# The first stage's channels stored in pairs and the slot spectra stored slot by slot, in a fused FFT, soft-MoE and SwiGLU kernel

## The chip, the core and the metric

The kernel runs on 1 core of one Trainium2 chip. The metric is device time in microseconds. Three runs of the kernel before took 1813.24, 1824.9 and 1827.48 us; their median is 1824.9 us. The engines are TensorE (PE; its weight loads are listed apart, as PEld), VectorE (DVE), ScalarE (ACT), GpSimd (POOL) and SyncE (SP), which issues most DMAs.

## The reference

Eight sequences of 3072 tokens of width 256 pass through three layers in turn.

```
X = rfft(x, axis=1)                             # x: [8, 3072, 256]
Yr = Xr @ w_r - Xi @ w_i + b_r ;  Yi = Xr @ w_i + Xi @ w_r + b_i
Y  = softshrink(Yr, 0.01) + 1j * softshrink(Yi, 0.01)
y  = irfft(Y)                                   # then [24576, 256]

logits = y @ phi                                # phi: [256, 32], 8 experts x 4 slots
d = softmax(logits, over all tokens);  c = softmax(logits, over the 32 slots)
slot_out[e] = relu((d.T @ y)[e] @ w1[e]) @ w2[e]
z = c @ slot_out

out = (silu(z @ w_gate) * (z @ w_val)) @ w_out  # 256 -> 1536 -> 256
```

All of it is in float32. The softmax over tokens runs over all eight sequences.

## The kernel before, in words

The 3072-point transform is split as 96 x 32. The first phase goes over the 8 batches b. For each:

- **Stage A** (`stage_a`): 16 products (L625) of the input with a 96-point transform; each gives one PSUM bank of 128 channels x 32 x 16 columns. A 32 x 32 block transpose on VectorE (L630) turns each bank into the tile `chan`, which has one slab of 128 columns per channel.
- **Stage C** (`stage_c`): per channel one product (L647) whose weights (the stationary operand) are that channel's 128 columns of `chan`; ScalarE and VectorE split the results into a high and a low part (L666, L669, L672, L675, L684, L688).
- **Stage B** (`stage_b`, L742): the mixing matrices w_r and w_i in three products per pair, on high and low parts. `after_b` does the shrinking (L795 to L814).
- **Stage Q** (`stage_q`): the logits' spectrum (L840), a transpose of it (L851), a transpose of Y in place (L856), and 16 DMAs (L866) that spread Y for the slots.
- **`logits`**: from the spectrum of 32 slots to logits over tokens, in two halves of 16 slots. Per half: product (L900), rotation by twiddle factors (L886, two multiplications), joins (L921), transpose (L929), product (L969), maximum (L978) and a copy kept for later (L990). The tile `vpad` is the transposes' source; it holds 24 rows of the ordinary pairs (`v_cj`) and, in row 24, the real pair (frequencies that have a real transform), copied in by L946.
- **`slots`**: the reverse way, from the exponentials to their spectrum: product (L1062), transpose (L1070), rotation (L886 on VectorE, the cross part on POOL or VectorE), joins (L1098), main product (`d_mm`, L1109), and for the real pair a small product of its own (`sd_mm`, L1119) in a PSUM bank of its own. `evac` copies the main product to SBUF (L1127) and then the real pair's 32 x 32 values over its place (L1130). Then `slot_mm` (L1163) forms the slots' inputs.
- **`combine`**: the softmax over slots, stored to DRAM.

In `vpad`, in the transposed tiles and in the logits, the slot is the innermost index: a half is 16 words in every 32.

The order of all this is not written by hand. Every step is a task handed to `Plan.add` with an engine, an estimated duration, a rank and the data it reads and writes. `Plan.run` is a list scheduler: among the tasks that can start it takes the one with the earliest estimated start, ties by rank, and emits it. The table `SHIFT` holds an offset of the rank for each kind of task. PSUM and SBUF buffers are rings with a fixed number of places (`ch`: 3 banks) and count as dependencies. Each engine then executes its own list strictly in order.

After the last batch, the expert weights that arrive by DMA are used (`after_slots`: L1513, L1536), and then the last layer runs over all 24576 tokens (L1614 to L1646), from about 742 us to the end.

Of the kernel before, what the change touches and what calls it, by code (L numbers as in the profile page):

```python
# [22 lines left out]
R1 = 96  # L23
# [9 lines left out]
def dft_tables():  # L33
# [64 lines left out]
    for i in range(R2):  # L98
        if i == 0:
            spi[0, 0, 0, :] = 1.0 / n  # L100
            spi[0, 1, 0, :] = alt2 / n
            spf[0, :, 0, 0] = 1.0 / n
            spf[0, :, 1, 0] = alt2 / n
# [7 lines left out]
        spf[h, :, 1, i] = -w * np.sin(a)  # L111

# [47 lines left out]
for _n, _w in (  # L160
# [59 lines left out]
    "slots.join": -7.11,  # L220
    "slots.sd_mm": -8.76,
    "slots.d_mm": -3.64,
# [44 lines left out]
    "slots.join'": 40.67,  # L267
    "slots.sd_mm'": 0.52,
    "slots.d_mm'": 14.24,
# [136 lines left out]
def kernel(  # L406
# [79 lines left out]
    def phase1():  # L486
# [39 lines left out]

        chan = apool.tile([128, 56, 128], F32, name="chan")

        twc = sm("twc").rearrange("p (c j) -> p c j", c=2)
        tws = sm("tws").rearrange("p (c j) -> p c j", c=2)  # L530
        inv = sm("inv").rearrange("p (m k) -> p m k", m=6)
# [3 lines left out]
        gf = sm("gf")  # L535
        v_cj = vpad[:, 0:24].rearrange("p (c j) s -> p c j s", c=2)

# [78 lines left out]
        def stage_a(b, p, rank):  # L616
            dq, dd = divmod(p, 4)
            dh, d0 = dq // 2, (dq % 2) * 64 + dd * 16
            kq = ("xq", b, dq) if b else ("x0", dh)
            kt, ka = ("tt", b, dh), ("ac", "a", b, p)  # L620
            d1 = dd * 16 if b else d0

            def mm():
                pt = bank(ka, [128, R2, 16], "ac")
                nc.tensor.matmul(  # L625
                    out=pt, lhsT=fwd[:, 8 - 8 * dh:136 - 8 * dh], rhs=T[kq][:, :, d1:d1 + 16], start=True, stop=True
                )

            def turn():
                nc.vector.transpose(  # L630
                    out=chan[:, 24 * dh:24 * dh + 32, d0:d0 + 16].rearrange("p j d -> p d j"),
                    in_=T[ka].rearrange("p n d -> p d n"),
                )

            add("PE", 0.86, rank, mm, r=["f", kq, kt], w=[ka], new=[("ac", ka)] + ([("tt", kt)] if p % 8 == 0 else []))
            add("DVE", 0.6, rank, turn, r=[ka], w=[(*kt, p)])

        def stage_c(b, g, hb, dh, rank):
# [51 lines left out]
            def last_mm():  # L690
                if dh == 0:
                    bank(kz, [128, 2, 2], "ch")
                nc.tensor.matmul(out=T[kz][:, dh], lhsT=chan[:, 32 * dh, :], rhs=sm("last"), start=True, stop=True)

# [189 lines left out]
        def times(eng, out, v, tw):  # L884
            e = nc.vector if eng == "DVE" else nc.gpsimd
            e.tensor_tensor(out=out, in0=v, in1=tw.unsqueeze(3).to_broadcast([128, 2, NSC, 16]), op=ALU.mult)  # L886

        half = [slice(0, 16), slice(16, 32)]

        def logits(b, k):  # L890
# [16 lines left out]
            def rot(h):  # L907
                def go():
                    if h == 0:
                        sb(chp, kp2, [128, 2, NSC, 32], "p2")  # L910
                    v = T["ch", "v", b, h]
                    times("DVE", v_cj[:, :, :, half[h]], v, twc)
                    times("DVE", T[kp2][:, :, :, half[h]], v, tws)

                return go

            def join(h):
                def go():
                    for c in range(2):
                        v = v_cj[:, c, :, half[h]]  # L920
                        nc.vector.tensor_add(out=v, in0=v, in1=T[kp2][:, 1 - c, :, half[h]])  # L921

                return go

            def turn(h):
                def go():
                    if h == 0:
                        sb(chp, kvt, [128, 32, 32], "vt")
                    nc.vector.transpose(  # L929
                        out=T[kvt][:, :, half[h]].rearrange("p n s -> p s n"),  # L930
                        in_=vpad[:, :, half[h]].rearrange("p m s -> p s m"),
                    )

# [11 lines left out]
            def sp_out():  # L945
                nc.scalar.activation(out=vpad[0:64, 24, :], in_=T[ks], func=AF.Copy)  # L946
# [19 lines left out]
            def l_mm(h):  # L966
                def go():
                    pt = bank(("ch", "l", b, h), [R1, 32, 16], "ch")
                    nc.tensor.matmul(out=pt, lhsT=gi, rhs=T[kvt][:, :, half[h]], start=True, stop=True)  # L969

                return go

            def colmax(h):
                def go():
                    if h == 0:
                        sb(chp, m96, [R1, 32], "m96")
                    pt = T["ch", "l", b, h].rearrange("p n s -> p s n")
                    nc.vector.reduce_max(out=T[m96][:, half[h]], in_=pt, axis=AX.X)  # L978

# [75 lines left out]
        def slots(b, k):  # L1055
# [10 lines left out]
            def turn(h):  # L1066
                def go():
                    if h == 0:
                        sb(chp, t2, [128, 32, 32], "vt")
                    nc.vector.transpose(  # L1070
                        out=T[t2][:, :, half[h]].rearrange("p m s -> p s m"),
                        in_=T["ch", "t", b, h].rearrange("p n s -> p s n"),
                    )

                return go

            def t4(h):
                return T[t2][:, 0:24, half[h]].rearrange("p (c j) s -> p c j s", c=2)

            def rot(h):  # L1080
                def go():
                    times("DVE", v_cj[:, :, :, half[h]], t4(h), twc)

                return go

            def cross(h):
                def go(eng):
                    if h == 0:
                        sb(chp, kp2, [128, 2, NSC, 32], "p2")
                    times(eng, T[kp2][:, :, :, half[h]], t4(h), tws)  # L1090

                return go

            def join(h):
                def go():
                    for c in range(2):
                        v = v_cj[:, c, :, half[h]]
                        nc.vector.tensor_sub(out=v, in0=v, in1=T[kp2][:, 1 - c, :, half[h]])  # L1098

                return go  # L1100

            ksd, d = ("ch", "sd", b), ("p2", "d", b)

            def d_mm(h):
                def go():
                    pt = bank(("ch", "d", b, h), [128, 2, NSC, 16], "ch")
                    for c in range(2):
                        for i in range(2):
                            nc.tensor.matmul(  # L1109
                                out=pt[:, c], lhsT=fwc[2 * c + i], rhs=v_cj[:, i, :, half[h]],  # L1110
                                start=(i == 0), stop=(i == 1),
                            )

                return go

            def sd_mm():
                pt = bank(ksd, [32, 2, 32], "ch")
                for c in range(2):
                    nc.tensor.matmul(  # L1119
                        out=pt[:, c], lhsT=spf[0:64, c, :], rhs=T[t2][0:64, 24, :], start=True, stop=True  # L1120
                    )

            def evac(h):
                def go():
                    if h == 0:
                        sb(chp, d, [128, 2, NSC, 32], "p2")
                    nc.scalar.activation(  # L1127
                        out=T[d][:, :, :, half[h]], in_=T["ch", "d", b, h], func=AF.Copy, scale=2.0 / SEQ
                    )
                    nc.scalar.activation(out=T[d][0:32, :, 0, half[h]], in_=T[ksd][:, :, half[h]], func=AF.Copy)  # L1130

                return go

            for h in range(2):
# [8 lines left out]
                add("DVE", 0.54, k + 0.01 * h, join(h), r=[(*kp2, h)], w=[("vp", h)])  # L1143
            add("PE", 0.1, k + 0.2, sd_mm, r=["csm", (*t2, 0), (*t2, 1)], w=[ksd], new=("ch", ksd))
            for h in range(2):
                kd = ("ch", "d", b, h)
                add("PE", 1.32, k + 0.2 + 0.01 * h, d_mm(h), r=["csm", ("vp", h)], w=[kd], new=("ch", kd), after=[ksd])
                add(
                    "ACT", 0.6, k + 0.2 + 0.01 * h, evac(h), r=[kd, ksd], w=[(*d, h)],
                    new=("p2", d) if h == 0 else None,  # L1150
# [553 lines left out]
```

## Time and profile before

| | |
|---|---|
| median of 3 runs | 1824.9 us (1813.24 to 1827.48) |
| profiled execution | 1821.86 us, its span 1819.8 us |
| TensorE busy in the span | 1719.7 us (94%) |
| VectorE busy | 1378.2 us (76%) |
| ScalarE busy | 984.8 us (54%) |
| POOL busy | 274.0 us (15%) |
| mean granted TensorE clock | 0.979 of full speed |

Busy time is the union of an engine's instructions. Averages over the span mix the first phase (to about 665 us), the change-over (to about 740 us) and the last layer, so the rows below are taken by stretch. A float32 product appears as two matmul records and two weight loads.

### The profile page before, as it was taken

The page shows a single profiled execution, that of the slowest core. Times are in us where ns is not written, and L with a number is a line of the kernel's source. Part 1 is how long each engine was busy: PE and PEld are TensorE (multiplying, and loading weights), DVE is VectorE, ACT ScalarE, POOL GpSimd, SP SyncE. Part 2 cuts the span into 40 slices and gives each one's busy share as a digit, 9 for nine tenths or more (in the row PEclk, how much of TensorE's full clock was granted, in tenths as well). Part 3 has the DMA queues.
Part 4 walks back from the last instruction along what each step waited for, and adds up shares of the span by engine and source line. Part 5 has one row for each costly group of instructions (what it writes and reads, how often), then busy time and mean ns, then how long its engine had stood idle before and what let it go on. Part 6 is the DMA issues. An engine that isn't in the chain of part 4 may idle for free.

```text
span 1819.8 us, 23377 instructions
## 1 busy us (share of the span) xinstructions
PE 1719.7 (94%) x8234; PEld 1291.9 (71%) x8234; DVE 1378.2 (76%) x2219; ACT 984.8 (54%) x1849; POOL 274.0 (15%) x257
## 2 busy tenths in 40 slices
PE   6999898997898996999999999999999999999998
PEld 3665655655565673688888888888888888888886
DVE  5798888898888872677777777777777777777776
ACT  1554545553553641565656565656565656565654
POOL 1324343442433342000000000000000000000000
PEclk8999989998999998999999999999999999999999
DMA  8355553755365569511211211211211212111111
GB/s 171 72 106 123 106 118 82 140 105 125 93 122 111 151 211 282 121 24 23 50 24 24 50 24 24 50 23 24 50 24 36 37 24 45 28 24 24 26 27 30
DMA packets 258916, 134.44 MB, mean 74 GB/s; under 512 B 197392, under 2 KB 246256, under 8 KB 258800
## 3 DMA queue, kind: packets, MB, share of 16 engines
q1 hardware_dynamic: 252944, 120.37, 31.3%
q0 software_dynamic: 5856, 12.58, 3.7%
q8 instruction: 65, 1.06, 0.3%
q14 instruction: 51, 0.42, 0.1%
HBM read 69.99 MB, written 37.75 MB: 59 GB/s over the span
## 4 chain that ended last, share of the span: by engine, by line
PE 74%; DVE 14%; DMA 4%; SPq 3%; issue 2%; ACT 2%; POOL 1%; DVEq 0%; ACTq 0%; POOLq 0%
PE o L1639 44%; PE pg L1614 7%; PE pv L1615 7%; PE pb L742 5%; PE ac L625 3%; PE ac L647 3%; DVE chan L630 3%; DMA w2s<-in_moe_w_dram 2%; DVE yt L856 1%; SPq L866 1%; DVE xg L669 1%; PE ch L840 1%; DVE vpad L1098 1%; DMA yi<-yt 1%; DVE vt L1070 1%
## 5 line engine op out<-in xcount | busy, mean ns | idle before, releaser
L1639 PE MATMUL o<-hh,wo 128*128 128x512 f32 x2304 | 722.5, 394 | 0.0
L1619 DVE TENSOR_TENSOR h<-sg,pv 128x512 f32<-128x512 f32 x576 | 394.0, 684 | 271.7 <-ACT sg L1617 270.1
L1617 ACT ACTIVATE sg<-pg 128x512 f32<-128x512 f32 x576 | 344.5, 598 | 421.8 <-PE pg L1614 421.8
L1639 PEld LDWEIGHTS o<-hh,wo 128*128 128x128 f32 x2304 | 434.3, 188 | 100.7
L1639 PE MATMUL o<-hl,wo 128*128 128x512 f32 x1152 | 453.9, 394 | 0.0
L1627 DVE TENSOR_TENSOR hl<-h,hh 128x512 fp32r<-128x512 f32 x576 | 393.4, 683 | 0.2
L1626 ACT ACTIVATE hh<-h 128x512 fp32r<-128x512 f32 x576 | 359.4, 624 | 0.7 <-DVE h L1619 0.7
L1639 PEld LDWEIGHTS o<-hl,wo 128*128 128x128 f32 x1152 | 216.1, 188 | 52.0 <-DVE hl L1627 0.2
L1614 PE MATMUL pg<-cst,gstk 96*128 96x512 f32 x576 | 228.3, 396 | 0.0
L1615 PE MATMUL pv<-cst,gstk 96*128 96x512 f32 x576 | 226.3, 393 | 0.7 <-DVE gstk L1601 0.7
L742 PE MATMUL pb<-xg,wh 128*128 128x512 f32 x384 | 150.5, 472 | 11.7 <-ACT yt L795 6.8
L814 POOL TENSOR_TENSOR yt<-r,yt 128x512 f32<-128x512 f32 x93 | 120.5, 1295 | 263.5 <-ACT yt L805 167.5
L630 DVE STREAM_TRANSPOSE chan<-ac 128x512 f32<-128x512 f32 x128 | 130.1, 1065 | 30.2 <-PE ac L625 30.1
L1566 POOL DMA_DIRECT2D cst<-c_scr x24 | 13.5, 571 | 813.1 <-PE pv L1615 799.7
L625 PE MATMUL ac<-xq,fwd 96*128 96x512 f32 x224 | 115.8, 628 | 14.5 <-DVE chan L630 9.2
L1615 PEld LDWEIGHTS pv<-cst,gstk 96*128 96x128 f32 x576 | 109.7, 190 | 27.3 <-DVE gstk L1601 1.6
L1614 PEld LDWEIGHTS pg<-cst,gstk 96*128 96x128 f32 x576 | 108.1, 188 | 24.4 <-issue 0.5
L647 PEld LDWEIGHTS ac<-cm,chan 128*128 128x128 f32 x768 | 96.7, 196 | 19.6 <-DVE chan L630 8.2
L647 PE MATMUL ac<-cm,chan 128*128 128x128 f32 x768 | 101.2, 282 | 5.9 <-DVE chan L630 3.3
L742 PEld LDWEIGHTS pb<-xg,wh 128*128 128x128 f32 x384 | 69.2, 197 | 51.1 <-issue 18.9
L669 DVE TENSOR_TENSOR xg<-ac,xg 128x512 fp32r<-128x512 f32 x96 | 64.8, 680 | 24.1 <-ACT sf L672 21.2
L625 PEld LDWEIGHTS ac<-xq,fwd 96*128 96x128 f32 x224 | 38.9, 194 | 58.7 <-DVE chan L630 33.4
(147 smaller groups left out, 1683.1 us busy)
## 6 DMA issues: line engine op xcount, KB each, us to landing
yi<-yt SPq DMA_DIRECT2D x384, 64.0 KB, 2.1
out_dram<-ob SPq DMA_DIRECT2D x192, 128.0 KB, 2.8
xq<-in_x_dram SPq DMA_DIRECT2D x28, 768.0 KB, 7.4
cst<-c_scr POOLq DMA_DIRECT2D x24, 384.0 KB, 6.7
w1s<-in_moe_w_dram SPq DMA_DIRECT2D x8, 1024.0 KB, 7.2
w2s<-in_moe_w_dram SPq DMA_DIRECT2D x8, 1024.0 KB, 10.3
w_scr<-cv SPq DMA_DIRECT2D x48, 128.0 KB, 2.2
x<-in_x_dram SPq DMA_DIRECT2D x2, 1536.0 KB, 15.0
```

The lines of the kernel that those rows point to most:

```text
L625: nc.tensor.matmul(out=pt, lhsT=fwd[:, 8 - 8 * dh:136 - 8 * dh], rhs=T[kq][:, :, d1:d1 + 16], start=True, stop=True)
L630: nc.vector.transpose(out=chan[:, 24 * dh:24 * dh + 32, d0:d0 + 16].rearrange("p j d -> p d j"), in_=T[ka].rearrange("p n d -> p d n"),)
L647: nc.tensor.matmul(out=pt[:, :, q:q + 2, i // 2, :], lhsT=chan[:, 32 * dh + j, :], rhs=cm[:, j, :].rearrange("p (c h k) -> p c h k", c=2, ...
L742: nc.tensor.matmul(out=pt, lhsT=w[:, dh, m, es], rhs=xx, start=m != 1 and dh == 0 and n == 0, stop=dh == 1 and n == 2, skip_group_check=True,)
L814: e.tensor_sub(out=part(), in0=quarters(T[kr]), in1=part())
L1614: nc.tensor.matmul(out=pg, lhsT=gstk[:, 0, f * 128:(f + 1) * 128], rhs=rhs, start=True, stop=True)
L1615: nc.tensor.matmul(out=pv, lhsT=gstk[:, 1, f * 128:(f + 1) * 128], rhs=rhs, start=True, stop=True)
L1617: nc.scalar.activation(out=sg, in_=pg, func=AF.Silu)
L1619: nc.vector.tensor_mul(out=h, in0=sg, in1=pv)
L1626: nc.scalar.activation(out=hh, in_=h, func=AF.Copy)
L1627: nc.vector.tensor_sub(out=hl, in0=h, in1=hh.bitcast(F32))
L1639: nc.tensor.matmul(out=po_t[0][k], lhsT=w[:, f % 4, k * 128:(k + 1) * 128], rhs=a, start=(f == 0 and m == 0), stop=(f == NF - 1 and m == 2 ...
```

## The change

Three things are done.

1. The tile `chan` becomes `[128, 28, 128, 2]`: the values of channels 2m and 2m+1 lie side by side. The transpose of stage A writes them in pairs; stage C takes one channel's weights with a step of two words.
2. In `logits` and `slots` the slot becomes the outer index: a half is 16 slots of 32 words without gaps, the transposes L929 and L1070 write without gaps, the rotation multiplies 16 x 24 words, and the joins handle 16 runs of 12 words. The logits in PSUM are also slot by slot; the copy L990 reads them across.
3. `sd_mm`, its bank and its tasks go. Its two products are done per half inside `d_mm` and added in the same PSUM bank, with the constants `spf` scaled to fit. The second copy of `evac` goes; the first reads its bank across.

The inverse product of batch b is given an order constraint after the `d_mm` of batch b - 1.

```diff
@@ dft_tables
-            spf[0, :, 0, 0] = 1.0 / n
+            spf[0, :, 0, 0] = 1.0 / w / n
...
-        spf[h, :, 0, i] = w * np.cos(a)
+        spf[h, :, 0, i] = np.cos(a)
@@ SHIFT: the two entries "slots.sd_mm" and "slots.sd_mm'" go
@@ tiles
-        chan = apool.tile([128, 56, 128], F32, name="chan")
+        chan = apool.tile([128, 28, 128, 2], F32, name="chan")
...
-        v_cj = vpad[:, 0:24].rearrange("p (c j) s -> p c j s", c=2)
+        v_cj = vpad[:, :, 0:24].rearrange("p s (c j) -> p s c j", c=2)
@@ stage_a
-                    out=chan[:, 24 * dh:24 * dh + 32, d0:d0 + 16].rearrange("p j d -> p d j"),
+                    out=chan[:, 12 * dh:12 * dh + 16, d0:d0 + 16, :].rearrange("p j d i -> p d j i"),
@@ stage_c
-                        out=pt[:, :, q:q + 2, i // 2, :], lhsT=chan[:, 32 * dh + j, :],
+                        out=pt[:, :, q:q + 2, i // 2, :], lhsT=chan[:, 16 * dh + j // 2, :, j % 2],
@@ times
-            e.tensor_tensor(out=out, in0=v, in1=tw.unsqueeze(3).to_broadcast([128, 2, NSC, 16]), op=ALU.mult)
+            e.tensor_tensor(out=out, in0=v, in1=tw.unsqueeze(1).to_broadcast([128, 16, 2 * NSC]), op=ALU.mult)
@@ logits
-                    v = T["ch", "v", b, h]
-                    times("DVE", v_cj[:, :, :, half[h]], v, twc)
+                    v = T["ch", "v", b, h].rearrange("p c j s -> p s (c j)")
+                    times("DVE", vpad[:, half[h], 0:24], v, twc)
...
-                        v = v_cj[:, c, :, half[h]]
-                        nc.vector.tensor_add(out=v, in0=v, in1=T[kp2][:, 1 - c, :, half[h]])
+                        v = v_cj[:, half[h], c]
+                        nc.vector.tensor_add(out=v, in0=v, in1=T[kp2][:, half[h], NSC * (1 - c):NSC * (2 - c)])
...
-                        out=T[kvt][:, :, half[h]].rearrange("p n s -> p s n"),
-                        in_=vpad[:, :, half[h]].rearrange("p m s -> p s m"),
+                    nc.vector.transpose(out=T[kvt][:, half[h]], in_=vpad[:, half[h]])
...
-                add("PE", 1.32, k + 0.01 * h, inv_mm(h), r=["csm"] + qts, w=[kv], new=("ch", kv))
+                add("PE", 1.32, k + 0.01 * h, inv_mm(h), r=["csm"] + qts, w=[kv], new=("ch", kv), after=[("ch", "d", b - 1, 1)] * (b > 0))
...
-                    nc.scalar.activation(out=T[ls][:, :, half[h]], in_=T["ch", "l", b, h], func=AF.Copy)
+                    nc.scalar.activation(out=T[ls][:, :, half[h]], in_=T["ch", "l", b, h].rearrange("p s n -> p n s"), func=AF.Copy)
@@ slots
-                        out=T[t2][:, :, half[h]].rearrange("p m s -> p s m"),
-                        in_=T["ch", "t", b, h].rearrange("p n s -> p s n"),
+                    nc.vector.transpose(out=T[t2][:, half[h]], in_=T["ch", "t", b, h].rearrange("p n s -> p s n"))
...
+                    for c in range(2):
+                        nc.tensor.matmul(
+                            out=pt[0:32, c, :, 0], lhsT=spf[0:64, c, :], rhs=T[t2][0:64, half[h], 24],
+                            start=False, stop=True, skip_group_check=True,
+                        )
...
-                    nc.scalar.activation(out=T[d][0:32, :, 0, half[h]], in_=T[ksd][:, :, half[h]], func=AF.Copy)
...
-            add("PE", 0.1, k + 0.2, sd_mm, r=["csm", (*t2, 0), (*t2, 1)], w=[ksd], new=("ch", ksd))
...
-                add("PE", 1.32, k + 0.2 + 0.01 * h, d_mm(h), r=["csm", ("vp", h)], w=[kd], new=("ch", kd), after=[ksd])
+                add("PE", 1.42, k + 0.2 + 0.01 * h, d_mm(h), r=["csm", ("vp", h), (*t2, h)], w=[kd], new=("ch", kd))
```

## Rows read from the trace of the kernel before

**Rows 1.** Windows: start:end, length, then busy us (instructions) per engine, granted clock, DMA.

```profile
core 0: us, PE busy (x) PEld busy (x) DVE busy (x) ACT busy (x) POOL busy (x), PEclk, DMA share, GB/s
26.00:665.00 639.00, 578.40 (x3151) 384.30 (x3151) 543.71 (x878) 324.52 (x669) 244.38 (x214) 0.95 0.53 115
665.00:740.00 75.00, 56.60 (x457) 35.27 (x453) 27.08 (x76) 14.37 (x26) 18.82 (x19) 0.91 1.00 281
742.00:1819.00 1077.00, 1071.40 (x4607) 867.69 (x4606) 794.98 (x1247) 642.36 (x1150) 10.01 (x18) 1.00 0.19 31
```

**Rows 2.** Chain of waits, 26 to 665 us: shares of the chain by engine and line.

```profile
by line: PE pb L742 14.8%; PE ac L625 9.4%; PE ac L647 9.1%; DVE chan L630 7.5%; issue 5.6%; DVE yt L856 4.2%; DVE xg L669 3.3%; PE ch L840 2.3%; SPq L866 2.1%; DVE vpad L1098 2.1%; DMA yi<-yt 2.1%; DVE vt L1070 2.0%; DVE yt L798 2.0%; DVE 
```

**Rows 3.** Waits of TensorE, 26 to 665 us: total us, times, longest us.

```profile
PE ac L625 <- DVE chan L630: 10.9, 14, 2.6
PE ch L969 <- DVE vt L929: 7.3, 5, 2.1
...
PE ac L647 <- DVE chan L630: 3.3, 4, 2.2
PE ch L969 <- DVE cv L1261: 3.1, 1, 3.1
```

**Rows 4.** Groups of VectorE by shape: busy us, mean ns of one, idle before them.

```profile
L630 DVE STREAM_TRANSPOSE chan<-ac 128x512 f32<-128x512 f32 x128 | 130.1, 1065 | 30.2 <-PE ac L625 30.1
...
L1646 DVE STREAM_TRANSPOSE ob<-o 128x512 f32<-128x512 f32 x96 | 62.7, 690 | 2.3 <-PE o L1639 2.3
L856 DVE STREAM_TRANSPOSE yt<-yt 128x1024 f32<-128x1024 f32 x48 | 58.5, 1219 | 6.1 <-PE ch L840 5.8
...
L929 DVE STREAM_TRANSPOSE vt<-vpad 128x512 f32<-128x512 f32 x16 | 18.6, 1161 | 0.8
...
L1070 DVE STREAM_TRANSPOSE vt<-ch 128x512 f32<-128x512 f32 x16 | 16.9, 1058 | 1.6 <-PE ch L1062 1.6
...
L978 DVE TENSOR_REDUCE m<-ch 96x16 f32<-96x512 f32 x16 | 10.6, 669 | 3.8 <-PE ch L969 3.7
L851 DVE STREAM_TRANSPOSE qt<-ch 128x256 f32<-128x256 f32 x24 | 10.3, 428 | 3.0 <-PE ch L840 3.0
...
L1219 DVE STREAM_TRANSPOSE vt<-ls 96x1024 f32<-96x1024 f32 x8 | 9.8, 1225 | 3.0 <-POOL ls L1215 3.0
```

**Rows 5.** Instructions of line L1098: min/median/max ns.

```profile
L1098 DVE TENSOR_TENSOR vpad<-vpad,p x32: 291/438/2062, 139.1 to 687.4; 128x192 f32<-128x192 f32 x32
```

**Rows 6.** Timeline of TensorE at 239 us: start, us, operation, idle before.

```profile
239.61 3.78 PE L625 MATMUL ac<-xq,fwd 96*128 96x512 f32 x4 [2.59 <-DVE chan L630]
```

**Rows 7.** Window of 240 to 250 us, columns as in the first group.

```profile
240.00:250.00 10.00, 10.00 (x24) 4.87 (x24) 7.59 (x11) 2.11 (x3) 2.99 (x2) 0.52 0.31 74
```

**Rows 8.** Timeline of TensorE and its weight loads: two stage C passes.

```profile
515.98 1.86 PEld L647 LDWEIGHTS ac<-cm,chan 128*128 128x128 f32 x16 [0.23 <-DVE chan L630]
...
641.18 1.95 PE L647 MATMUL ac<-cm,chan 128*128 128x128 f32 x16
```

**Rows 9.** Groups of ScalarE by shape, columns as for VectorE.

```profile
L684 ACT ACTIVATE sg<-sf 128x256 fp32r<-128x256 f32 x96 | 37.4, 413 | 27.6 <-PE pb L742 24.6 <-DVE sf L675 2.7
...
L1267 ACT ACTIVATE cvi<-cvi 128x256 f32<-128x256 f32 x36 | 15.9, 442 | 37.7 <-DVE cv L1262 33.9 <-issue 3.8
```

**Rows 10.** Timeline of TensorE at 138 us.

```profile
138.38 0.31 PE L1119 MATMUL ch<-vt,csm 64*32 64x32 f32 x4 [0.93 <-DVE vt L1070]
```

**Rows 11.** Groups of ScalarE: the copies out of PSUM in logits and slots.

```profile
L990 ACT ACTIVATE ls<-ch 96x512 f32<-96x512 f32 x16 | 9.5, 591 | 30.6 <-DVE m L978 30.5
...
L1127 ACT ACTIVATE p<-ch 128x384 f32<-128x384 f32 x16 | 7.8, 489 | 19.5 <-DVE vpad L1098 8.6 <-PE ch L1109 8.3 <-PE pb L742 2.5
...
L1130 ACT ACTIVATE p<-ch 32x32 f32<-32x32 f32 x16 | 3.0, 186 | 0.5
```

**Rows 12.** Groups of VectorE: the logits' rotation.

```profile
L886 DVE TENSOR_TENSOR p<-ch,csm 128x384 f32<-128x384 f32 x16 | 8.8, 549 | 0.0
```

**Rows 13.** Timeline of TensorE at 724 us.

```profile
724.59 4.99 PE L1536 MATMUL po<-w2s,h1t 128*32 128x256 f32 x58 [9.80 <-DMA w2s<-in_moe_w_dram]
```

More of the change, by code (lines that the diff above doesn't have):

```diff
@@ L101, in dft_tables @@
             spi[0, 1, 0, :] = alt2 / n
-            spf[0, :, 0, 0] = 1.0 / n
-            spf[0, :, 1, 0] = alt2 / n
+            spf[0, :, 0, 0] = 1.0 / w / n
+            spf[0, :, 1, 0] = alt2 / w / n
             continue
@@ L220 @@
     "slots.join": -7.11,
-    "slots.sd_mm": -8.76,
     "slots.d_mm": -3.64,
@@ L267 @@
     "slots.join'": 40.67,
-    "slots.sd_mm'": 0.52,
     "slots.d_mm'": 14.24,
@@ L525, in phase1 @@
         fwd = apool.tile([R1, FWD], F32, name="fwd")
-        chan = apool.tile([128, 56, 128], F32, name="chan")
-        twc = sm("twc").rearrange("p (c j) -> p c j", c=2)
-        tws = sm("tws").rearrange("p (c j) -> p c j", c=2)
+        chan = apool.tile([128, 28, 128, 2], F32, name="chan")
+        twc = sm("twc")
+        tws = sm("tws")
         inv = sm("inv").rearrange("p (m k) -> p m k", m=6)
@@ L692, in last_mm @@
                     bank(kz, [128, 2, 2], "ch")
-                nc.tensor.matmul(out=T[kz][:, dh], lhsT=chan[:, 32 * dh, :], rhs=sm("last"), start=True, stop=True)
+                nc.tensor.matmul(out=T[kz][:, dh], lhsT=chan[:, 16 * dh, :, 0], rhs=sm("last"), start=True, stop=True)
             def last_out():
@@ L909, in go @@
                     if h == 0:
-                        sb(chp, kp2, [128, 2, NSC, 32], "p2")
-                    v = T["ch", "v", b, h]
-                    times("DVE", v_cj[:, :, :, half[h]], v, twc)
-                    times("DVE", T[kp2][:, :, :, half[h]], v, tws)
+                        sb(chp, kp2, [128, 32, 2 * NSC], "p2")
+                    v = T["ch", "v", b, h].rearrange("p c j s -> p s (c j)")
+                    times("DVE", vpad[:, half[h], 0:24], v, twc)
+                    times("DVE", T[kp2][:, half[h]], v, tws)
                 return go
@@ L945, in sp_out @@
             def sp_out():
-                nc.scalar.activation(out=vpad[0:64, 24, :], in_=T[ks], func=AF.Copy)
+                nc.scalar.activation(out=vpad[0:64, :, 24], in_=T[ks], func=AF.Copy)
             for h in range(2):
                 kv = ("ch", "v", b, h)
-                add("PE", 1.32, k + 0.01 * h, inv_mm(h), r=["csm"] + qts, w=[kv], new=("ch", kv))
+                add("PE", 1.32, k + 0.01 * h, inv_mm(h), r=["csm"] + qts, w=[kv], new=("ch", kv), after=[("ch", "d", b - 1, 1)] * (b > 0))
                 if h == 0:
@@ L967, in go @@
                 def go():
-                    pt = bank(("ch", "l", b, h), [R1, 32, 16], "ch")
-                    nc.tensor.matmul(out=pt, lhsT=gi, rhs=T[kvt][:, :, half[h]], start=True, stop=True)
+                    pt = bank(("ch", "l", b, h), [R1, 16, 32], "ch")
+                    nc.tensor.matmul(out=pt, lhsT=gi, rhs=T[kvt][:, half[h]], start=True, stop=True)
                 return go
@@ L976, in go @@
                         sb(chp, m96, [R1, 32], "m96")
-                    pt = T["ch", "l", b, h].rearrange("p n s -> p s n")
-                    nc.vector.reduce_max(out=T[m96][:, half[h]], in_=pt, axis=AX.X)
+                    nc.vector.reduce_max(out=T[m96][:, half[h]], in_=T["ch", "l", b, h], axis=AX.X)
                 return go
@@ L1069, in go @@
                         sb(chp, t2, [128, 32, 32], "vt")
-                    nc.vector.transpose(
-                        out=T[t2][:, :, half[h]].rearrange("p m s -> p s m"),
-                        in_=T["ch", "t", b, h].rearrange("p n s -> p s n"),
-                    )
+                    nc.vector.transpose(out=T[t2][:, half[h]], in_=T["ch", "t", b, h].rearrange("p n s -> p s n"))
                 return go
             def t4(h):
-                return T[t2][:, 0:24, half[h]].rearrange("p (c j) s -> p c j s", c=2)
+                return T[t2][:, half[h], 0:24]
             def rot(h):
                 def go():
-                    times("DVE", v_cj[:, :, :, half[h]], t4(h), twc)
+                    times("DVE", vpad[:, half[h], 0:24], t4(h), twc)
                 return go
@@ L1088, in go @@
                     if h == 0:
-                        sb(chp, kp2, [128, 2, NSC, 32], "p2")
-                    times(eng, T[kp2][:, :, :, half[h]], t4(h), tws)
+                        sb(chp, kp2, [128, 32, 2 * NSC], "p2")
+                    times(eng, T[kp2][:, half[h]], t4(h), tws)
                 return go
@@ L1096, in go @@
                     for c in range(2):
-                        v = v_cj[:, c, :, half[h]]
-                        nc.vector.tensor_sub(out=v, in0=v, in1=T[kp2][:, 1 - c, :, half[h]])
+                        v = v_cj[:, half[h], c]
+                        nc.vector.tensor_sub(out=v, in0=v, in1=T[kp2][:, half[h], NSC * (1 - c):NSC * (2 - c)])
                 return go
-            ksd, d = ("ch", "sd", b), ("p2", "d", b)
+            d = ("p2", "d", b)
             def d_mm(h):
                 def go():
-                    pt = bank(("ch", "d", b, h), [128, 2, NSC, 16], "ch")
+                    pt = bank(("ch", "d", b, h), [128, 2, 16, NSC], "ch")
                     for c in range(2):
@@ L1109, in go @@
                             nc.tensor.matmul(
-                                out=pt[:, c], lhsT=fwc[2 * c + i], rhs=v_cj[:, i, :, half[h]],
-                                start=(i == 0), stop=(i == 1),
-                            )
-                return go
[L1116 to L1121, printed above, removed]
+                                out=pt[:, c], lhsT=fwc[2 * c + i], rhs=v_cj[:, half[h], i],
+                                start=(i == 0), stop=(i == 1), skip_group_check=True,
+                            )
+                    for c in range(2):
[3 more added lines that the diff above has]
+                        )
+                return go
             def evac(h):
@@ L1127, in go @@
                     nc.scalar.activation(
-                        out=T[d][:, :, :, half[h]], in_=T["ch", "d", b, h], func=AF.Copy, scale=2.0 / SEQ
+                        out=T[d][:, :, :, half[h]], in_=T["ch", "d", b, h].rearrange("p c s j -> p c j s"),
+                        func=AF.Copy, scale=2.0 / SEQ,
                     )
-                    nc.scalar.activation(out=T[d][0:32, :, 0, half[h]], in_=T[ksd][:, :, half[h]], func=AF.Copy)
                 return go
```

6 lines of the change are left out of this document (2 added, 4 removed).

## The prediction

> **What bounds the kernel now.** I read the busy time by stretch first [rows 1]. The long last stage, 742 to 1819 us, keeps TensorE busy for 1071.4 of 1077 us, and no line of it is edited: the change can only act before it. From 26 to 665 us the eight batches of the first phase run, and two engines are nearly full at once: TensorE 578.4 and VectorE 543.7 of 639 us. Neither can be named the bound alone. Between them, 665 to 740, the DMA engines are busy all the time (share 1.00).
>
> The chain of waits inside 26 to 665 us [rows 2] says how the two share the end. TensorE has the largest pieces (L742 14.8%, L625 9.4%, L647 9.1%), but the stage A transpose L630 alone holds 7.5%, and the slots' transpose L1070 2.0%. The waits of TensorE [rows 3] agree: the longest single total is for L630, and the third transpose, L929, costs it 7.3 us in 5 waits.
>
> **The transposes.** In the groups of VectorE [rows 4] the same operation of 512 columns has two prices: 690 ns where it writes without gaps (L1646), and 1065 (L630), 1161 (L929) and 1058 (L1070) where each word lands 128 or 512 bytes from the last. From L851 (256 columns, 428 ns) and L1646 a gapless one costs 166 ns + 1.02 ns per column; the 1024 columns of L1219 and L856, read from SBUF, fit that at 1219 to 1225, so the source does not matter. It is the write that costs, not the gapped read: the reduction L978 reads PSUM at 64 byte steps, as L630 and L1070 do, and takes 669 ns for 512, no more than gapless work of that size. A gapped write costs (1065 - 166)/512 = 1.76 ns per word.
>
> - L929 and L1070 get outputs without gaps: I take 690, so 0.47 and 0.37 us less, 16 times each, 13.4 us of VectorE. The other end is nothing gained.
> - L630 now writes two words side by side and then jumps 1024 bytes. No row has pairs. The upper bound is 1065, the lower 690. In between: were the 0.73 ns extra per jump simply added, a pair would pay it once, 1.02 + 0.37 = 1.39 ns per word, 878 ns. I take 690: a jump costs 1.76 ns in all, and the two words need 2.04 ns in any case, so it fits under them; and the joins L1098, which jump after every 16 words, have a fastest execution of 291 ns for 192 words [rows 5], under the 362 of 166 + 1.02 x 192, so a jump by itself is not charged. That is 128 x 0.375 = 48 us of VectorE.
>
> The Trainium skill, "SBUF — State Buffer", section "Door 1: The DMA port swizzle", says that accesses which keep moving to a new 16-byte line pay, and that two hits on a line are enough to hide it. By that rule the pair is at 690 and the sum is the one below; without any such effect L630 stays at 1065 and the sum loses 16.9 us. No row here shows which.
>
> **What of it lies on the path.** L630: 7.5% of 639 us is 47.9 us on the chain; 375/1065 of that is 16.9. L1070: 2.0% is 12.8, times 368/1058 is 4.4. L929 is not named in the chain's line; of the 7.3 us in 5 waits each can lose at most 0.47, so 2.4. Together 23.7 us. With the order of work unchanged the chain cannot shrink by more, and other chains lie close behind, since TensorE is already busy 90.5% of the stretch. I take four fifths, 19 us: it would leave TensorE busy 578/620 = 93%. Half is the pessimistic end.
>
> **The clock.** TensorE loses speed after long waits. At 239.6 us it had waited 2.59 us for L630, and four stage A matmul records took 3.78 us [rows 6]; the granted clock from 240 to 250 is 0.52, the lower level of 1.2 GHz [rows 7]. Over 26 to 665 us the mean is 0.95 [rows 1], so 0.05 x 639 = 32 us of full-speed time is lost. Shorter waits for L630 give some back. Bounds 0 to 16 us (half); I take 4, as the two waits for L630 (10.9 + 3.3 us) and the one for L929 are 21.5 of the 60.6 us in which TensorE is idle, and they shorten by about a third.
>
> **The weights of stage C.** L647 loads its weights from the channel tile, now with a step of 8 bytes. No weight load of this trace has a step. Today 16 records take 1.86 us on the load side and 1.95 on the matmul side [rows 8], 0.11 us each: load and matmul are level, nothing would hide a slower load. Lower bound: no change. Upper bound: twice the load, 0.11 us x 768 = 85 us of TensorE. I take no change, by the nearest row with such a step: ScalarE squares 256 words in place at 8 byte steps in 442 ns, against 413 for 256 words without gaps [rows 9].
>
> **The small matmuls of the slots.** One set of four records becomes two per batch, 0.31 us each [rows 10]: 8 x 0.31 = 2.5 us of TensorE at most; below, 0, if they run beside others. TensorE holds some 40% of the chain: +1 us. They wait only for the transposes that the main product needed already. The new order constraint (inverse product after the last batch's spectra) changes nothing: both lie on TensorE, and the products stand in that order in the trace.
>
> **ScalarE.** The second copy of the slots' evacuation goes, 16 x 0.186 = 3.0 us; the first (L1127, 489 ns) and the copy of the logits (L990, 591 ns) now read PSUM with gaps [rows 11]. Bounds: 0, or the same 0.73 ns per word as a gapped write, 16 x (0.28 + 0.37) = 10.4 us. ScalarE is busy 324.5 of 639 us [rows 1], which covers it; without that cover, net +7. I take 0.
>
> **Rotations and joins.** The logits' rotation reads PSUM at 64 byte steps: 0 by L978, else 32 x 0.28 = 9 us of VectorE over 549 ns each [rows 12]. The joins write runs of 12 words for 16; 0 by the 291 ns. Both taken as 0. POOL's cross product keeps its size and stays on the same task.
>
> **The tail.** The last batch's logits and slots also get shorter, but there TensorE waits 9.80 us for the expert weights afterwards [rows 13], a transfer released by the end of the batches. Gain 0; without that cover about 1.7 us.
>
> **Sum.** -19 - 4 + 1 = -22 us. The profiled execution took 1821.9 us (span 1819.8, 2.1 around it), 3.0 below the median of 1824.9; 1821.9 - 22 = 1800.
>
> **Rivals.**
> - **TensorE takes over as the bound.** For it: 90.5% busy. Against: VectorE holds much of the chain. Half of 23.7 is realised and no clock: -12 + 1, 1811.
> - **The pairs do nothing.** The change then saves only in L929 and L1070: (4.4 + 2.4) x 0.8 = 5, less 1: 1818. For it: no row has pairs. Against: the reading of the 291 ns.
> - **The stepped weight load is slow, the result slower.** Place: L647. 9.1% of 639 is 58.1 us on the chain; doubled loads add that much, less the 22: 1822 + 58 - 22 = 1858. It decides from where it eats the 22 us: 22/58 of 0.11, some 0.04 us more per load. For it: load and matmul are level. Against: ScalarE's row.
> - **The planner's new order.** Removing a task and its bank shifts the order that a list of hand offsets steers, from the first slots on. If each batch gains one wait like the 3.1 us for L1261 [rows 3], 8 x 3.1 = 25 us: 1825.
>
> **Numbers.** Forecast 0.56, its own range 1782 (all 23.7 and 16 of clock) to 1816 (half, no clock, and the extra VectorE and ScalarE work partly on the path); TensorE as the bound 0.15; pairs idle 0.10; slow weights 0.11; order 0.08. The range 1780 to 1830 leaves out the slow weights and the ends of the rest, under 2 in 10. About 1% (18 us) is what this measurement can tell from no change: below 1806.7 lie three quarters of the forecast, a third of the second case and, should the new order happen to be a better one, part of the last, 0.42 + 0.05 + 0.03 = 0.50. Slower by 1%: the weights, and a little of the order, 0.13. The rest, 0.37, is within.
>
> **What would show it.** In the groups of VectorE: L630 near 690 (or 878, or 1065), L929 and L1070 at 690. The L647 loads still 0.11 us apart. TensorE's waits for L630 shorter and the mean clock above 0.95. Busy VectorE down by 61 us to about 480. Wrong would be: L647's records further apart, transposes unchanged, or transposes at 690 with TensorE idle as long as before, behind another line.

## The result and the profile after

The changed kernel takes 1791.4 us (median of 4 runs, 1787.02 to 1794.86) against 1824.7 for the kernel before (now four runs): ratio 0.9833, 95% interval 0.9806 to 0.9861, so 30 us less by the ratio, 25 to 35. The forecast was 1800 us. Its profiled execution took 1793.57 us, 28.3 below that of before.

The first batches end with the first of the idle products that keep TensorE occupied after the last stage B. The timeline of TensorE, before and after:

```profile
657.80 1.06 PE L1465 MATMUL pb<-ident 128*128 128x128 f32 x8
```

```profile
624.33 1.28 PE L1454 MATMUL pb<-ident 128*128 128x128 f32 x10
```

The eight batches end 33.5 us earlier. Of that, 3.3 us were lost again in the change-over, as the start of the last layer's gates moved from 731.4 to 701.2 us, and 1.8 in the last layer (1088.4 and 1090.2 us). Windows from 26 us to the end of the batches, of the kernel before and of the changed one (columns as in [rows 1]):

```profile
26.00:657.80 631.80, 571.20 (x3084) 378.14 (x3085) 539.99 (x872) 321.37 (x664) 241.27 (x212) 0.95 0.53 115
```

```profile
26.00:624.30 598.30, 560.09 (x3111) 384.31 (x3112) 489.60 (x862) 316.51 (x645) 238.93 (x206) 0.97 0.56 121
```

VectorE is busy 50.4 us less. TensorE's idle time fell from 60.6 to 38.2 us and its busy time by 11.1, although it now has more weight loads. That part goes with the clock, 0.95 to 0.97, from 5% of 632 (32 us) to 3% of 598 (18 us) of full-speed time lost. TensorE was busy 90.4% of this stretch and is now busy 93.6%. In the change-over the clock went the other way: 0.91 over 73.6 us before, 0.84 over 76.9 us now, so 7 us of full-speed time lost became 12.

The groups of VectorE, which answer to [rows 4]:

```profile
L628 DVE STREAM_TRANSPOSE chan<-ac 128x512 f32<-128x512 f32 x128 | 88.7, 703 | 35.7 <-PE ac L623 32.7
...
L927 DVE STREAM_TRANSPOSE vt<-vpad 128x512 f32<-128x512 f32 x16 | 11.4, 711 | 0.8
L1064 DVE STREAM_TRANSPOSE vt<-ch 128x512 f32<-128x512 f32 x16 | 11.0, 686 | 0.0
L972 DVE TENSOR_REDUCE m<-ch 96x16 f32<-96x512 f32 x16 | 10.8, 673 | 2.5 <-PE ch L964 2.4
...
L884 DVE TENSOR_TENSOR p<-ch,csm 128x384 f32<-128x384 f32 x16 | 8.7, 545 | 0.0
```

All three transposes are near the gapless price of 690 ns: the pairs (L628, was L630) at 703, L927 at 711, L1064 at 686. L1064 still reads PSUM at 64 byte steps and pays nothing: the write was the cost. The logits' rotation (L884) reads PSUM that way too, 545 ns against 549 in [rows 12].

The groups of ScalarE, which answer to [rows 11]; there is no second copy any more:

```profile
L984 ACT ACTIVATE ls<-ch 96x512 f32<-96x512 f32 x16 | 9.5, 591 | 10.3 <-DVE m L972 10.3
...
L1117 ACT ACTIVATE p<-ch 128x384 f32<-128x384 f32 x16 | 7.8, 489 | 40.4 <-PE ch L1106 22.6 <-DVE vpad L1089 17.5
```

Reading PSUM across costs ScalarE nothing: 591 and 489 ns, as before. The group of the stage C weight loads, before and after, and the timeline of loads and products after, to be held against [rows 8]:

```profile
L647 PEld LDWEIGHTS ac<-cm,chan 128*128 128x128 f32 x768 | 96.7, 196 | 19.6 <-DVE chan L630 8.2 <-issue 3.8 <-DVE xg L669 3.7
```

```profile
L645 PEld LDWEIGHTS ac<-cm,chan 128*128 128x128 f32 x768 | 100.6, 200 | 17.7 <-issue 6.4
...
43.43 2.08 PEld L645 LDWEIGHTS ac<-cm,chan 128*128 128x128 f32 x16
43.66 2.04 PE L645 MATMUL ac<-cm,chan 128*128 128x128 f32 x16
```

16 records take 2.04 us on the matmul side, for 1.95: a load at a step of 8 bytes costs some 6 ns more, 48 x 0.09 = 4 us in all.

The chain of waits inside 26 to 624 us, which answers to [rows 2]:

```profile
by line: PE pb L740 19.5%; PE ac L623 12.8%; PE ac L645 10.3%; issue 3.8%; DVE yt L854 3.4%; PE ch L838 2.9%; DVE xg L667 2.9%; PE ch L1152 2.8%; PE ch L1100 2.6%; DVE chan L628 2.4%; DVE cv L1251 2.3%; DVE vpad L884 2.2%; DVE sf L673 2.0%;
```

The stage A transpose went from 7.5% of the chain to 2.4%, and what took its place is TensorE's own work. The waits of TensorE, 26 to 640 us, which answer to [rows 3] (the batches end 33 us earlier, so the stretch is shorter):

```profile
PE ch L1100 <- DVE vpad L1089: 8.5, 6, 5.0
PE ac L623 <- DVE chan L628: 5.3, 5, 2.2
...
PE ch L964 <- DVE vt L927: 2.8, 4, 1.7
...
PE ac L645 <- DVE chan L628: 1.5, 2, 1.1
```

The three waits for transposes came to 21.5 us and are 9.6. A new one leads: the spectra's product (L1100) for the joins (L1089). It comes with the new order and not with the layouts: the kernel before waits there for 2.7 us, the fold alone (below), in the old layouts, for 9.0.

### The profile page after: what moved, and what is told of

It reads as the page before. It is cut to its first block, busy times and chain, and to the rows that moved or that the text cites. A ratio compares the mean times of both kernels' runs of the same rounds, so it can differ in the third digit from the quotient of the medians.

```text
span 1791.4 us, 23405 instructions
## 1 busy us (share of the span) xinstructions
PE 1710.6 (95%) x8266; PEld 1300.9 (73%) x8266; DVE 1329.6 (74%) x2222; ACT 981.4 (55%) x1833; POOL 275.0 (15%) x254
## 4 chain that ended last, share of the span: by engine, by line
PE 81%; DVE 12%; DMA 1%; issue 1%; SPq 1%; ACT 1%; POOL 0%; DVEq 0%; ACTq 0%
PE o L1628 45%; PE pg L1603 7%; PE pv L1604 7%; PE pb L740 7%; PE ac L623 4%; PE ac L645 3%; PE ch L1100 1%; DVE yt L854 1%; PE ch L1152 1%; PE ch L838 1%; DVE xg L667 1%; DVE cv L1251 1%; DVE chan L628 1%; DVE vpad L884 1%; PE pb L1454 1%
## 5 line engine op out<-in xcount | busy, mean ns | idle before, releaser
L623 PE MATMUL ac<-xq,fwd 96*128 96x512 f32 x224 | 111.4, 606 | 4.6 <-DVE chan L628 2.4
L628 DVE STREAM_TRANSPOSE chan<-ac 128x512 f32<-128x512 f32 x128 | 88.7, 703 | 35.7 <-PE ac L623 32.7
L645 PEld LDWEIGHTS ac<-cm,chan 128*128 128x128 f32 x768 | 100.6, 200 | 17.7 <-issue 6.4
L645 PE MATMUL ac<-cm,chan 128*128 128x128 f32 x768 | 105.6, 288 | 3.2 <-DVE xg L667 1.7
L667 DVE TENSOR_TENSOR xg<-ac,xg 128x512 fp32r<-128x512 f32 x96 | 64.9, 680 | 23.7 <-ACT sf L670 14.8
L740 PE MATMUL pb<-xg,wl 128*128 128x512 f32 x192 | 77.1, 401 | 0.0
```

The costliest lines, as they stand in the source:

```text
L623: nc.tensor.matmul(out=pt, lhsT=fwd[:, 8 - 8 * dh:136 - 8 * dh], rhs=T[kq][:, :, d1:d1 + 16], start=True, stop=True)
L628: nc.vector.transpose(out=chan[:, 12 * dh:12 * dh + 16, d0:d0 + 16, :].rearrange("p j d i -> p d j i"), in_=T[ka].rearrange("p n d -> p d n"),
L645: nc.tensor.matmul(out=pt[:, :, q:q + 2, i // 2, :], lhsT=chan[:, 16 * dh + j // 2, :, j % 2], rhs=cm[:, j, :].rearrange("p (c h k) -> p c ...
L740: nc.tensor.matmul(out=pt, lhsT=w[:, dh, m, es], rhs=xx, start=m != 1 and dh == 0 and n == 0, stop=dh == 1 and n == 2, skip_group_check=True,)
```

## The experiments

The theory, called D in the expectations: shorter transposes, and the clock they give back, make all of the gain, and I under-estimated the chain. Its rival, O: my sum is right as long as the order is unchanged, and the rest came with the new order that the planner made once the real pair's task was gone. A third, W, came up on the way: the saved copies did it. The third part of the change, the real pair's products done inside the main product, is called the fold here. The planner makes the separation clean. Its tasks do not depend on the layouts, so the layouts alone keep every engine's list of before, and the fold alone has the lists of the changed kernel.

**Pairs alone.** In the kernel before:

```diff
-        chan = apool.tile([128, 56, 128], F32, name="chan")
+        chan = apool.tile([128, 28, 128, 2], F32, name="chan")
...   (with the writes and reads of the change)
```

> The kernel before with the channel tile in pairs alone; every engine's list of instructions is in the order of before. Theory D (shorter transposes and the clock they give back explain the whole gain, the chain was under-estimated): about -25 us against before, 1800. Theory O (my sum is right for an unchanged order, and the rest comes from the new order that the planner made): 0.8 x 16.9 + 3 of clock = -17 us, 1808, and not below 1800. Both expect the stage A transpose at 703 ns and the weight loads of stage C some 6 ns further apart than before, as in the changed kernel.

Measured: 0.9925 (0.9905 to 0.9946), 1808.45 us, 14 us less (10 to 17). The transposes take 702 ns. The time fits O's 1808, and the interval leaves out D's 25 us.

**The slot-by-slot layout alone** (rotations, joins, transposes and copies as in the change; the real pair stays a task of its own).

```diff
-                    nc.tensor.matmul(out=pt, lhsT=gi, rhs=T[kvt][:, :, half[h]], start=True, stop=True)
+                    nc.tensor.matmul(out=pt, lhsT=gi, rhs=T[kvt][:, half[h]], start=True, stop=True)
...
-                    out=pt[:, c], lhsT=spf[0:64, c, :], rhs=T[t2][0:64, 24, :], start=True, stop=True
+                    out=pt[:, c], lhsT=spf[0:64, c, :], rhs=T[t2][0:64, :, 24], start=True, stop=True
```

> The kernel before with the slot-by-slot layout alone (the real pair's product and second copy stay); order of before. Theory D: -8 us, 1817. Theory O: 0.8 x (4.4 + 2.4) = -5 us, 1819. Rival in both: ScalarE pays for reading PSUM across in the logits' copy, which the changed kernel's 591 ns already speaks against: then nothing or slower.

Measured: 0.9954 (0.9936 to 0.9972), 1813.11 us, 8 us less; nearer to D's 8 than to O's 5, and the interval (5 to 12) holds both.

**Both layouts, old order.**

> Pairs and slot-by-slot layout together, the real pair as before; order of before. Theory D: the whole gain, 1788 to 1796. Theory O: the sum of my prediction, -22 us, 1798 to 1806, so that some 9 us are left for the fold and its order.

Measured: 0.9880 (0.9857 to 0.9902), 1797.82 us, 22 us less (18 to 26): my sum without the small products, as O says, though the median itself lies just under O's 1798. The two layouts add up (14 + 8). Against the whole change, 30 us by the ratio, some 8 us are missing. In the profiles the changed kernel is 12 us ahead of this one at the end of the batches (624.3 and 636.4) and 5 at the start of the gates (701.2 and 706.6).

**The fold alone**, in the old layouts, in the order of the changed kernel.

```diff
+                            out=pt[0:32, c, 0, :], lhsT=spf[0:64, c, :], rhs=T[t2][0:64, 24, half[h]],
+                            start=False, stop=True, skip_group_check=True,
...
-            add("PE", 0.1, k + 0.2, sd_mm, r=["csm", (*t2, 0), (*t2, 1)], w=[ksd], new=("ch", ksd))
```

> The kernel before with the real pair's products added in the main product's bank and the second copy gone, in the old layouts; every engine's list is in the order of the changed kernel. Theory D: nothing, 1821 to 1828. Theory O: the new order and the saved copies alone give 6 to 12 us, 1813 to 1819.

Measured: 0.9945 (0.9925 to 0.9966), 1811.98 us, 10 us less (6 to 14). D falls: the part that I had put at +1 gains 10. Its window:

```profile
26.00:640.70 614.70, 560.56 (x3111) 375.66 (x3112) 528.88 (x862) 316.31 (x645) 237.01 (x206) 0.98 0.55 117
```

Against the kernel before, TensorE is idle 54.1 us (60.6) and busy 10.6 us less, with small products added. The granted clock is 0.98 for 0.95. So this order loses less time at the lower level. But this profile is the fastest of the six runs (1807.31 us, clock 0.987 over the whole span). Over all six the mean clock is 0.9835, against 0.9808 in the eleven of the kernel before beside them: 30 us of full-speed time lost for 35, so about half of the 10 us.

**The second copy left out**, nothing else, in the kernel before.

```diff
-                    nc.scalar.activation(out=T[d][0:32, :, 0, half[h]], in_=T[ksd][:, :, half[h]], func=AF.Copy)
```

> The kernel before with the second copy of the slots' evacuation left out (16 x 0.186 us of ScalarE; the real pair's share of the slots' inputs is left out of the result); TensorE's list is that of before, instruction for instruction, and ScalarE's lacks those 16. The fold alone was 10 us faster than before. Theory O (the new order does that): nothing here, 1820 to 1824. Rival W (the saved copies, which stand between the spectra and the slots' product, do it): 6 to 10 us, 1812 to 1816.

Measured: 0.9965 (0.9952 to 0.9979), 1817.56 us, 6 us less (4 to 9): the size that W gives, against O's "nothing", though the median lies above W's 1816. Whether it is more than the copies' own 3.0 us is not shown. The kernel before was run anew in four sets beside these experiments, with medians of 1819.45, 1822.01, 1822.35 and, beside this kernel, 1824.51 us; and the profile of this kernel ends its batches at 660.8 us, no earlier than before (657.8).

**The copy kept, but not from the real pair's bank.**

```diff
-                    nc.scalar.activation(out=T[d][0:32, :, 0, half[h]], in_=T[ksd][:, :, half[h]], func=AF.Copy)
+                    nc.scalar.activation(out=T[d][0:32, :, 0, half[h]], in_=T["ch", "d", b, h][0:32, :, 0, :], func=AF.Copy)
```

> The kernel before with the second copy kept at its place and size, but taken from the main product's bank instead of the real pair's (the real pair's share of the slots' inputs is left out of the result); all engines' lists are those of before. Left out altogether, the copy had given 4 to 9 us. Theory T (ScalarE's time for the copy): nothing here, 1820 to 1825. Theory B (the bank of the real pair, held until the second copy, and the wait that goes with it): 4 to 9 us again, 1813 to 1818. If neither stands out, the fold's 10 us stay with the order.

Measured: 1.0006 (0.9990 to 1.0022), 1822.25 us. The bank is not it. What is left is ScalarE's time for the copy, by elimination. The waits show little of it: in the profile before, TensorE's products wait for the copy once, 0.8 us (L1163 for L1130).

**The copy put back into the changed kernel.**

```diff
+                    nc.scalar.activation(
+                        out=T[d][0:32, :, 0, half[h]], in_=T["ch", "d", b, h][0:32, :, :, 0], func=AF.Copy, scale=2.0 / SEQ
+                    )
```

> The changed kernel with the second copy put back (the same 32 x 32 values copied once more out of the main product's bank, 16 x 0.186 us of ScalarE); TensorE's list is unchanged. Leaving the copy out of the kernel before gave 4 to 9 us. Theory W (the copy itself is on the path, between spectra and slots' product): 1795 to 1800. Rival B (it was the real pair's own bank, which the copy kept occupied, or the order): within 3 us of 1791.

Measured: 0.9822 (0.9804 to 0.9841), 1786.52 us: no price that can be told, 2 us faster than the changed kernel by the ratios, which ran on another occasion; the two intervals together leave room for some 4 us. W's 1795 to 1800 did not come. So the copy explains at most a part of what the fold is worth in the changed kernel. That it costs 6 us in the one order and nothing in the other is what the medians say, and it is not clear of their spread.

**Other orders for the same work.** The changed kernel with the offsets of the slots' tasks drawn anew by up to 6, twice; TensorE's lists differ from the changed kernel's about as widely as that of the kernel before does.

> The changed kernel with the planner's hand offsets of the slots' tasks moved by up to 6 at random: the same work, and TensorE's list differs in about as many rows from the changed kernel's as that does from before. Theory O: order alone moves the time by several us either way, 1785 to 1805, and a random one is more likely slower than 1791. Rival W: within 3 us of 1791.

Measured: 0.9854 (0.9840 to 0.9868), 1796.45 us.

> As the one before, with another draw of the offsets. Theory O: 1785 to 1805 and different from the first draw by more than 3 us. Rival W: within 3 us of 1791.

Measured: 0.9898 (0.9883 to 0.9913), 1805.55 us. By the ratios these are 4 and 12 us slower than the changed kernel, with the same work, and 8 apart from each other; the 4 are within the intervals. Order alone can be worth as much as the fold. It moves time between stretches, too: in the first draw's profile the batches end at 639.7 us, 15 later than in the changed kernel, and the gates start at 701.8, where those of the changed kernel do (701.2).

**Fours instead of pairs**, on the changed kernel.

```diff
-        chan = apool.tile([128, 28, 128, 2], F32, name="chan")
+        chan = apool.tile([128, 14, 128, 4], F32, name="chan")
...
-                        out=pt[:, :, q:q + 2, i // 2, :], lhsT=chan[:, 16 * dh + j // 2, :, j % 2],
+                        out=pt[:, :, q:q + 2, i // 2, :], lhsT=chan[:, 8 * dh + j // 4, :, j % 4],
```

> The changed kernel with the channels in fours: the transpose writes four words side by side, the weights of stage C are read at a step of 16 bytes. Theory R (the step costs in proportion to the lines of 16 bytes it touches, which is what would follow from the Trainium skill, page 'SBUF - State Buffer', section on the port swizzle): the loads now hit a new line each and slow down well beyond the 6 ns of the pairs, by 50 to 110 ns each, TensorE's stage C grows by 40 to 85 us and the kernel is slower than 1815. Rival S (a small fixed price of any step): loads stay within 10 ns of the pairs, the transpose goes from 703 to 690 ns, time 1788 to 1795.

Measured: 1.0218 (1.0203 to 1.0233), 1863.01 us, slower than before. Groups of that kernel:

```profile
L645 PE MATMUL ac<-cm,chan 128*128 128x128 f32 x768 | 187.9, 397 | 2.5 <-DVE chan L628 1.4 <-DVE xg L667 1.0
L645 PEld LDWEIGHTS ac<-cm,chan 128*128 128x128 f32 x768 | 185.2, 327 | 14.7 <-DVE chan L628 5.0 <-issue 4.8 <-DVE xg L667 1.1
L628 DVE STREAM_TRANSPOSE chan<-ac 128x512 f32<-128x512 f32 x128 | 89.0, 704 | 37.2 <-PE ac L623 34.5
```

and its timeline of the loads:

```profile
45.97 3.81 PEld L645 LDWEIGHTS ac<-cm,chan 128*128 128x128 f32 x16
```

The transpose gains nothing over pairs (704 for 703 ns), while 16 loads take 3.81 us for 2.08. Loads with a step of 16 bytes cost 327 ns, with 8 bytes 200, without a step 196. That is my rival of the slow weights, at the next step size, and my price for it (0.11 us per load, 85 us in all) is the 85 us by which the loads' busy time grew, 100.6 to 185.2. Of it, 72 us reached the time (1863.01 for 1791.37), where the rival had 58 by L647's share of the chain. The Trainium skill, "SBUF — State Buffer", section "Door 1: The DMA port swizzle", says that two accesses on a 16-byte line hide the change of line. The trace agrees in all three: pairs written at 703 ns, loads at 8 bytes nearly free (200 ns for 196), loads at 16 bytes not (327 ns).

**The stall after the batches.** In the changed kernel the change-over has a wait that the kernel before has not; that one waits 9.80 us for w2 instead [rows 13]. Its timeline, VectorE and TensorE:

```profile
678.56 0.29 DVE L1250 TENSOR_SCALAR cv<-cvi 128x256 int32<-128x256 int32 x1 [11.15 <-DMA w_scr<-cv]
...
680.27 0.22 DVE L1490 COPY tail<-pst 128x64 f32<-128x64 f32 x1
...
680.55 4.24 PE L1502 MATMUL ph<-w1s,tail 128*32 128x512 f32 x20 [14.86 <-DVE tail L1493]
```

The planner left the last w_out tile to be narrowed until here; VectorE waits for the store of the one before, and the copy that the expert products need stands behind it. Two kernels try to remove it: two buffers for those tiles (order unchanged), and an earlier offset for their loads (a new order).

```diff
-                t = sb(chp, ki, [128, 256, 2], "cvi", dt=I32)
+                t = sb(chp, ki, [128, 256, 2], "cvi", 2, dt=I32)
...   (the same for "cva" and "cvp")
```

> The changed kernel with two buffers instead of one for the w_out tiles that are narrowed (three SBUF tiles); order of all engines unchanged. In the changed kernel's trace VectorE waits 11.15 us at 678 us for the store of such a tile, and behind it, in order, stands the copy that the expert products need; TensorE waits 14.86 us. Theory V (that stall gave back part of the gain): TensorE's wait falls to 6 us or less and the kernel takes 1782 to 1787. Rival M (the expert weights' transfers end the change-over anyway): 1789 to 1793, with the wait moved to the products that need w2.

Measured: 0.9809 (0.9790 to 0.9828), 1786.03 us. Run beside it, the kernel with the copy put back (1786.52) has the single buffers, so this is no gain that can be told apart. TensorE's wait is still there:

```profile
682.23 5.72 PE L1502 MATMUL ph<-w1s,tail 128*32 128x512 f32 x32 [11.14 <-DVE tail L1493]
```

Neither expectation holds as a whole: the time lies in the range of V, but the wait did not fall to 6 us, nor did it move to the products that need w2. With two buffers VectorE's wait before L1250, at 680.23 us, is 7.45 us, and it is for the last tile itself to arrive (`cvi` from `w_out`) and no longer for the store.

```diff
-    "narrow.load": 18.5,
+    "narrow.load": 6.0,
```

> The changed kernel with the planner's offset for the narrowing's loads at 6 instead of 18.5, so that the last narrowed tile comes 22 instructions ahead of that copy on VectorE, not 4; the order changes elsewhere too. Theory V with a neutral order: 1782 to 1790. Theory O (any new order costs): 1794 to 1805.

Measured: 0.9935 (0.9917 to 0.9954), 1808.8 us, some 18 us slower than the changed kernel. TensorE now waits for w2 instead, as in the kernel before:

```profile
713.62 5.49 PE L1525 MATMUL po<-w2s,h1t 128*32 128x256 f32 x58 [8.31 <-DMA w2s<-in_moe_w_dram]
```

and the batches end at 647.8 us for 624.3. O again, and beyond its 1805: the new order cost more than the stall. No version tried beats the changed kernel beyond its interval.

## Why the prediction was right, and where a term was not

The side, the range and the size of the forecast hold: 30 us by the ratio for a forecast of 25 from the median. The sum itself was 22; the other 3 are the distance of the profiled execution from the median. So the sum lacks some 8 us, and the experiments put them on one term, the fold. That the planner's new order fell on the good side was luck. By the steps of the prediction:

- **Transposes.** Taken at 690 ns; 703, 711 and 686. Their busy time fell from 165.6 to 111.1 us, 54.5 of the 61 forecast. That the write and not the read costs is shown by L1064, and the choice of the full rate for pairs by 703.
- **Rotations and joins.** Taken as 0. The logits' rotation (545 ns) and the joins (L1089, 575 ns for 703; L919, 486 for 502) bear it out. The slots' rotation does not: with the same lists, the fold alone against the changed kernel, it went from 593 to 777 ns on VectorE and from 1151 to 1275 on POOL, 16 times each, so 3 and 2 us that the sum lacks. Why is not shown.
- **The path.** "With the order of work unchanged the chain cannot shrink by more" than 23.7 us, four fifths taken, 4 added for the clock. With the order of before, both layouts gave 22 us (18 to 26), for 19 + 4. Pairs alone: 0.8 x 16.9 = 13.5 forecast without the clock, 14 measured. The slots' part was larger, 8 for 5, within its interval.
- **Small products, copy and order.** This is the term that was mis-sized, "+1" and "I take 0" for ScalarE: the fold gave 10 us. I counted the removed copies as covered because ScalarE is busy only half of the time; in the order of before, leaving them out gave 6 us (4 to 9). And I priced the planner's new order only as a rival that loses 25 us, with 8 in 100; that it might be a better one got 3 of these and no size. Random orders lost 4 and 12, another 18; of the four orders tried for this work the planner's own is the fastest.
- **The clock.** Taken at 4 of 0 to 16 us; the time lost in the batches went from 32 to 18 us in the profiles. With both layouts and the old order it is 4% of 610, 24 us. One profile bears only so much, though. Over the whole span, with the change-over, the mean clock is 0.9845 in the four runs of the changed kernel and 0.9812 in the 48 of the kernel before that ran beside the experiments: 28 us lost for 34, so 6 us, near the 4 forecast. The windows of both layouts, and then of two more kernels with TensorE's list of the changed one, the copy put back and the two buffers:

```profile
26.00:636.40 610.40, 565.56 (x3084) 382.11 (x3084) 501.95 (x871) 320.89 (x664) 243.92 (x212) 0.96 0.55 119
```

```profile
26.00:621.40 595.40, 557.12 (x3112) 382.64 (x3113) 489.40 (x862) 318.83 (x659) 238.98 (x206) 0.98 0.56 121
```

```profile
26.00:629.70 603.70, 565.40 (x3111) 386.14 (x3112) 489.42 (x862) 316.36 (x645) 238.82 (x206) 0.96 0.56 120
```

VectorE is busy the same 489.4 us in the last two, and their batches end 8 us apart with the clock; so the clock's share in the fold cannot be taken from one profile to better than that.
- **Weights.** Taken as unchanged; 6 ns each, 4 us of TensorE that the sum lacks. The rival's price was right for a step of 16 bytes.
- **TensorE as the bound.** Held at 0.15: half the gain and no clock. It did not come, yet the profile after looks like it: TensorE busy 93.6%, 93% forecast, and the chain's largest lines its own.
- **The tail.** Forecast to give nothing; in the profiles it took 3.3 us back. The stall above, which no step had, stands where the 9.80 us for w2 had stood. That it made the 3.3 us is not shown: the kernel with the copy put back has the same stall (13.53 us), and its change-over took 72.7 us, less than the 73.6 before.

What stays open: how the fold's 10 us divide between the copy, the order and the clock. No kernel has the folded products in the order of before, and the copy's price, 6 us in one order and none that can be told in the other, may depend on the order.

## What to carry to other kernels

Write what a transpose scatters in runs of two float32 words, and read it back at a step of two: both sides are then near the full rate (703 ns for 690, loads 6 ns longer), while one word costs the writer and four cost the weight loads. With instruction lists made by a planner, separate a change's durations from its order by building the parts that leave the planner's tasks alone; here three quarters of the gain came with the old list, and the same work in other lists varied by 4 to 18 us. Do not put an instruction at nothing because its engine is half idle: look at what is queued behind it, and measure with it left out.

## What I had not expected of the hardware

- VectorE writes float32 at the full rate in runs of two words (703 ns for 512 columns, 704 in runs of four), and TensorE's weight loads bear a step of two words but not of four: 200 and 327 ns.
- 16 copies of 0.186 us, 3.0 us of ScalarE in all [rows 11], gave 6 us (4 to 9) when left out in the order of before, and cost nothing that can be told when put into the changed kernel. Whether that is more than the 3.0 is not shown.
- Three kernels with the same list of TensorE ended their batches at 621.4, 624.3 and 629.7 us in their profiles, with granted clocks of 0.98, 0.97 and 0.96. The spread of single runs, 1813 to 1827 us before, is of that size.
